# A new slot plan for banded attention followed by a gated MLP: masks of two sessions added as a bias, v of the fourth batch loaded behind its q and k, another split of one weight load

## The chip, the cores and the metric

The kernel runs on one core of a Trainium2 chip. The time is that of one execution on the device, in microseconds (us); before the change its median over three runs is 303.94 us (303.85 to 304.52). The engines are named as in the profile: PE multiplies matrices (PEld loads its weights), DVE and ACT work elementwise, POOL and SP issue DMAs here, and POOL also does a few copies.

## What is computed

Eight batches of eight heads with 576 positions of 64 dimensions go through attention in a band of 32 positions to each side; the result, as 4608 tokens of 512, goes through two matrices with a smooth ReLU between them.

```python
scores = scale * np.matmul(q, k.transpose(0, 1, 3, 2))
mask = np.abs(pos[:, None] - pos[None, :]) <= window        # window = 32
scores = np.where(mask, scores, -1000000000.0)
...
attn = attn / (np.sum(attn, axis=-1, keepdims=True) + 1e-09)
x = np.matmul(attn, v)            # as (4608, 512)
h = x @ w_in                      # (512, 2048)
g = np.where(pos, h, np.where(neg, 0.0, (h + beta) ** 2 / (4.0 * beta)))
return g @ w_out                  # (2048, 512)
```

## The kernel before

**Slots.** The program is a list of 144 slots (the loop over `a`). Each slot does one piece of the first projection: a tile `hp` of 128 x 512 sums in PSUM, either 256 of the 2048 inner columns for 256 tokens (eight matmuls of 256 columns, line 609) or, in slots 56 to 135, 128 inner columns for 512 tokens (four matmuls of 512 columns, line 630). ACT then computes `rr` from it (line 648), and the gate is finished in one of two ways: DVE does two operations (lines 654 and 655), or, for the slots listed in `two_on_act`, ACT does a square (line 651) and DVE one operation (line 652). `hp` has two buffers (pool `ps_h`), so the tile of slot a can be begun when that of slot a-2 has been read for the last time. That is after line 654 in the first way and after line 652 in the second.

**What lies between the slots.** The second projection fills PE's time. It comes as `pair` (lines 573 to 588: eight matmuls of 256 columns, numbered 0 to 15, for the first 512 tokens, placed by the list `pairs`) and as `unit` (one matmul of 512 columns, line 563, so many per slot as `units` says). Sixteen units make an output tile of 128 tokens, which is copied out of PSUM by DVE or ACT (line 567) and stored. Pairs 0, 1, 2, 3 read the four parts `('o', 0, 0, 4)` to `('o', 0, 12, 16)` of w_out; each pair also needs the gates of the slots whose inner columns it reads.

**Attention.** For batch 0 there are functions of its own (`scores`, `sums`). Batches 1 to 7 are a stream of 23 turns: `stream_scores(k)` multiplies q and k in quarters of the array (line 283), takes the exponential on ACT (lines 289, 292), multiplies by the band mask on DVE (line 200) and adds two halves into `rows` on DVE (lines 299 to 303). `stream_sums(k)` multiplies by v and by ones (line 366), ACT takes the reciprocal of the sums by a logarithm and an exponential (lines 317 to 321), and DVE multiplies into `xT` (line 325), which is what the first projection reads. Where they stand is a list of (position, names); position 12.5 lies behind the pairs and units of slot 12, position 13.0 ahead of those of slot 13. At a position listed in `ends_first` the reciprocal goes ahead of the scores that follow; elsewhere behind them. Two banks of PSUM each are held by the pools `ps_s` and `ps_n`.

**A mask in two ways.** `mask(eng, ...)` multiplies on DVE. Where `eng` is None, nothing is multiplied, and `add_mask` (line 202) has put a large negative bias into the PSUM banks by four matmuls of 512 columns ahead of the scores, which then add to it. `bias_until` is the position up to which the second way is taken; `stream_scores` knows only the first.

**Loads.** POOL issues the loads in the order of `LOADS`, written by hand: w_in in parts (`'w'`), w_out in parts (`'o'`), q and k of batch 1 (`'rows'`), v of batch 1, the two copies that make `mask4` (`'masks'`, lines 151 and 153, no DMA), and q and k of batch 2 (`'nat'`). Batch 0 and 1 are transposed by PE (`tposes`; `tq` and `tk` are those of q and k of batch 1). From batch 2 on, q and k are loaded by `load_nat` (line 103), transposed by a DMA that SP issues (`xpose`, line 193), and after the transpose of k POOL makes a copy of two columns of it into `gate` (line 668), so that the four loads of v (line 111) that are behind it are issued when that transpose has landed. The q and k of the next batch are behind them on POOL, and their buffers are those of the batch before.

The load of columns 256 to 512 of w_in into the lower 64 partitions is divided after 52 of its 64 rows.

Of the kernel before, what the change touches and what calls it, by code (L numbers as in the profile page):

```python
# [14 lines left out]
def kernel(  # L15
# [59 lines left out]
    qTs = [const.tile([128, PAD + NY * S], BF, name=f"qT{i}") for i in range(3)]  # L75

    ctx.enter_context(tc.manual_schedule())
    LOADS = [('v', 0, 1), ('v', 0, 2), ('v', 0, 3), ('w', 0, 256, 0), ('w', 0, 256, 1), ('w', 256, 512, 0), ('w', 256, 512, 1, (0, 52, 64)), ('half', 1, 0, 0), ('half', 1, 0, 1), ('half', 1, 1, 0), ('half', 1, 1, 1), ('w', 512, 768, 0), ('w', 512, 768, 1), ('w', 768, 1024, 0), ('w', 768, 1024, 1), ('w', 1024, 1280, 0), ('w', 1024, 1280, 1), ('w', 1280, 1536, 0), ('w', 1280, 1536, 1), ('w', 1536, 2048, 0), ('w', 1536, 2048, 1), ('o', 0, 0, 4), ('o', 0, 4, 8), ('o', 0, 8, 12), ('rows', 1, 0), ('rows', 1, 1), ('o', 0, 12, 16), ('v', 1, 0), ('v', 1, 1), ('v', 1, 2), ('v', 1, 3), ('masks',), ('o', 1, 0, 8), ('o', 1, 8, 16), ('nat', 2, 0), ('nat', 2, 1)]
    V, P, A = nc.vector, nc.gpsimd, nc.scalar


# [110 lines left out]

# [71 lines left out]

    def stream_scores(k, eng, pool=ps_s):

        assert eng is not None
        s, gs = turns[k]
        m = len(gs)
        r0 = (gs[0] - s) % TURN  # L270
        ps = two_banks(pool)
        sp = list(spare()) if m == 3 else None

        def place(h, y, n):
            return sp[h][:, 1, 128 * y:128 * y + 128] if n == 2 else ps[:, h, 256 * y + 128 * n:256 * y + 128 * n + 128]

        for y, n in [(y, n) for y in range(2) for n in range(min(m, 2))] + [(y, 2) for y in range(2) if m == 3]:
            for a in range(2):
                for h in range(2):
                    b, c = 1 + gs[n] // NC, gs[n] % NC  # L280
                    lo, hi = 32 * (c == 0), TAIL if c == NC - 1 else 128
                    s0 = S * (y + 2 * a) + 64 * c
                    nc.tensor.matmul(place(h, y, n)[HD[a], lo:hi], kT[b][HD[h], s0:s0 + 64],  # L283
                                     qTs[b % 3][HD[h], PAD + s0 - 32 + lo:PAD + s0 - 32 + hi],
                                     start=True, stop=True, skip_group_check=True)
        w0 = 128 * r0
        lo, hi = 32 * (gs[0] % NC == 0), 128 * m - 32 * (gs[-1] % NC == NC - 1)
        cut = min(hi, 256)
        A.activation(wt[:, :, w0 + lo:w0 + cut], ps.rearrange("p h (y j) -> p (h y) j", y=2)[:, :, lo:cut], AF.Exp,  # L289
                     scale=D ** -0.5)  # L290
        for h in (1, 0) if m == 3 else ():
            A.activation(wt[:, 2 * h:2 * h + 2, w0 + 256:w0 + hi],  # L292
                         sp[h][:, 1].rearrange("p (y j) -> p y j", y=2)[:, :, :hi - 256], AF.Exp, scale=D ** -0.5)
        mask(eng, wt[:, :, w0 + lo:w0 + hi], mask4.rearrange("p (m j) -> p m j", m=4)[:, :, lo:hi])
        M = turn_of(k)
        r = rows[64 * gs[0] - 32] = ptp.tile([128, 4, 192], BF, name="rows", bufs=2)
        if r0:
            x = wt[:, :, w0 - 64:w0 - 64 + 128 * M].rearrange("p m (n e j) -> p m n e j", n=M, e=2)
            V.tensor_add(r[:, :, :64 * M].rearrange("p m (n j) -> p m n j", n=M), x[:, :, :, 0], x[:, :, :, 1])
# [202 lines left out]

    NB = NT // TB
    NF = DFF // 256
    pairs = [(7, 0), (7, 1), (8, 2), (11, 4), (12, 5), (13, 3), (15, 8), (15, 6), (17, 9), (17, 7), (18, 10), (20, 11), (21, 14), (22, 12), (23, 15), (23, 13)]
    ev = {}

    def at(a, *todo):
# [7 lines left out]
                   "s1": (sums, 0, 1, TB, MAIN), "s2": (sums, 0, 0, MAIN, S, ps_s),  # L516
                   "tq": (tposes, 1, (0, 0), (0, 1)), "tk": (tposes, 1, (1, 0), (1, 1)),
                   "C1": (*seq[1][1], ps_n), "C3": (*seq[3][1], ps_n), "S2": (*seq[2][0], ps_s), "S0": (*seq[0][0], ps_s)}
    for a, *names in [(1, 't0'), (2, 'c0', 'c2'), (3, 'c1', 's0'), (4, 's1'), (5, 's2'), (10, 'tq'), (11.5, 'tk'), (12.5, (1, 0), 'C1'), (14.5, 'S0', (0, 1)), (15.5, (1, 2)), (19, (0, 2), (1, 3)), (21.5, (0, 3)), (24, (1, 4))]:
        for x in names:  # L520
            at(a, early_items[x] if isinstance(x, str) else seq[x[1]][x[0]])
    two_on_act = [1, 7, 10, 11, 12, 13, 25, 35, 41, 46, 53, 61, 68, 73, 75, 83, 88, 89, 90, 93, 96, 97, 104, 108, 110, 112, 113, 124, 125, 128, 129, 130, 131, 132, 133, 134, 135, 138, 139, 142, 147, 150, 152, 157]
    sl = [26.0, 29, 33, 36, 39, 44, 48, 51, 59, 66, 71, 74, 81, 87, 95, 99, 108, 111, 123]
    first_sl = 4
    bias_until = 12
    ends_first = [14, 14.5, 15.5, 16, 20, 21.5, 24.5, 27, 28, 34, 37, 38, 40, 42, 45, 46, 49, 50, 52, 54, 55, 57, 58, 62, 63, 67, 68, 69, 73, 76, 77, 78, 80, 84, 86, 88, 90, 91, 93, 94, 96, 97, 98, 101, 103, 104, 106, 110, 112, 114, 117, 120, 121, 122, 127, 130, 132, 134]
    for n, a in enumerate(sl):
# [11 lines left out]
    op = {}  # L539
# [5 lines left out]
    def unit(x):  # L545
# [70 lines left out]
    units = [0, 0, 0, 0, 0, 0, 0, 0, 0, 0, 0, 0, 0, 0, 0, 0, 0, 0, 0, 0, 0, 0, 1, 0, 0, 0, 2, 2, 5, 4, 2, 7, 2, 6, 1, 8, 7, 0, 8, 7, 2, 6, 2, 1, 5, 3, 7, 1, 6, 3, 6, 3, 4, 8, 2, 2, 2, 2, 2, 4, 4, 7, 2, 2, 2, 2, 6, 4, 5, 2, 1, 4, 2, 9, 7, 0, 9, 2, 3, 2, 2, 6, 4, 5, 2, 2, 2, 4, 4, 9, 2, 5, 0, 5, 2, 5, 5, 6, 2, 3, 4, 8, 3, 1, 3, 4, 0, 4, 6, 6, 5, 4, 3, 9, 2, 2, 2, 2, 4, 2, 8, 0, 5, 5, 0, 8, 1, 5, 0, 7, 1, 6, 1, 6, 1, 6, 1, 6, 1, 7, 3, 4, 3, 65, 2, 2, 1, 0, 0, 0, 0, 0, 0, 0, 0, 0, 0, 0, 0, 0]  # L616
    for a in range(NF * NB + 2 * NF):
        wide = WIDE[0] <= a < WIDE[1]
        for b, x in loads.get(a, []):
            load_nat(b, x)  # L620
        if a == 0 or a > 3:
            flush()
        if a < NF * NB:
# [40 lines left out]
        run(a + 0.5)  # L664
        for x in xps.get(a, []):
            xpose(*x)
            if x[1]:
                P.tensor_copy(gate, qkT(x[0], 1)[:, 0:2])  # L668
                for n in range(4):
                    load_v(x[0], n)  # L670
# [30 lines left out]
```

## Time and profile before

| what | value |
|---|---|
| median of three runs | 303.94 us |
| the profiled execution: its time | 304.81 us |
| its span, first to last instruction | 303.0 us |
| granted clock of PE | 0.999 |
| PE busy | 293.1 us (97%), 3244 matmuls |
| DVE busy | 232.0 us (77%) |
| ACT busy | 203.4 us (67%) |
| POOL busy | 78.8 us (26%) |
| DMA issued by POOL (`q0`) | 18.06 MB |

Times inside the profile count from the start of the span. A line of the timeline gives the start, the length from the first start to the modelled end of the last, the engine, the line of the kernel, output and inputs, the shape, how many instructions are merged, and in brackets how long the engine was idle before and what released it. Matmuls overlap, so the length of a row of eight (1.04 us) is longer than its distance to the next row (0.87 us); the distance between starts is what counts.

### The profile page before, as it was taken

What the parts mean: (1) busy time and instruction counts of PE and PEld (TensorE: products, weight loads), DVE (VectorE), ACT (ScalarE), POOL (GpSimd) and SP (SyncE); (2) the same over time, 40 slices, a digit from 0 to 9 for tenths busy, and PEclk for the clock granted to TensorE, in tenths of its full rate; (3) what the DMA queues carried; (4) which work ended last, traced back from release to release, by engine and by line L of the source; (5) the groups of instructions that cost most, each with busy time, mean ns of one, the idle gap of its engine ahead of it and who ended that gap; (6) DMA issues with size and microseconds to landing.
All of it is one profiled execution on the core that took longest, in us unless ns stands there. A gap on an engine that the chain in (4) does not pass through costs nothing.

```text
span 303.0 us, 7769 instructions
## 1 busy us (share of the span) xinstructions
PE 293.1 (97%) x3244; PEld 172.2 (57%) x3244; DVE 232.0 (77%) x361; ACT 203.4 (67%) x383; POOL 78.8 (26%) x98
## 2 busy tenths in 40 slices
PE   8788999999999999999999999999999999999995
PEld 3466888876665766644444444444444444446644
DVE  4269789989987889898988989688978887546700
ACT  3678696757786777766878487777578547685301
POOL 8794740090073046055046000050000000000000
PEclk9999999999999999999999999999999999999999
DMA  9999999999999999999989900697111110000121
GB/s 151 180 180 199 187 186 154 225 151 156 185 65 147 178 171 145 166 188 147 195 119 161 159 17 22 131 137 73 38 35 38 35 37 35 37 35 35 38 104 69
DMA packets 137971, 35.66 MB, mean 118 GB/s; under 512 B 122320, under 2 KB 134352, under 8 KB 137936
## 3 DMA queue, kind: packets, MB, share of 16 engines
q0 software_dynamic: 103056, 18.06, 81.0%
q1 hardware_dynamic: 34736, 16.81, 23.9%
q8 instruction: 25, 0.41, 0.6%
q10 hardware_dynamic: 144, 0.29, 0.4%
q14 instruction: 10, 0.08, 0.1%
HBM read 36.70 MB, written 9.44 MB: 152 GB/s over the span
## 4 chain that ended last, share of the span: by engine, by line
PE 82%; DMA 7%; POOL 5%; DVE 2%; ACT 2%; issue 1%; POOLq 0%; ACTq 0%; DVEq 0%
PE op L563 34%; PE hp L630 23%; PE hp L609 14%; PE op L581 4%; PE bb L366 3%; DMA w_out<-in_moe_w_out_dram 3%; DMA vn<-in_v_dram 2%; POOL w_in L116 2%; DMA w_in<-in_moe_w_in_dram 2%; POOL vn L111 2%; PE bb L283 1%; PE op L554 1%; DVE wt L200 1%; PE tp L186 1%; PE sp L366 1%
## 5 line engine op out<-in xcount | busy, mean ns | idle before, releaser
L648 ACT ACTIVATE rr<-hp 128x512 f32<-128x512 f32 x144 | 84.9, 594 | 67.0 <-PE hp L630 36.1
L563 PE MATMUL op<-w_out,gT 128*128 128x512 bf16 x496 | 125.5, 380 | 0.0
L654 DVE TENSOR_TENSOR mx<-hp,rr 128x512 f32<-128x512 f32 x104 | 71.2, 685 | 17.2 <-ACT rr L648 16.5
L630 PE MATMUL hp<-xT,w_in 128*128 128x512 bf16 x320 | 81.1, 379 | 0.0
L563 PEld LDWEIGHTS <-gT 128*128 128x128 bf16 x496 | 46.9, 98 | 49.8
L655 DVE SCALAR_TENSOR_TENSOR gT<-rr,mx 128x512 bf16<-128x512 f32 x104 | 72.2, 694 | 3.6
L609 PE MATMUL hp<-xT,w_in 128*128 128x256 bf16 x512 | 65.8, 273 | 2.6 <-DMA w_in<-in_moe_w_in_dram 1.7
L609 PEld LDWEIGHTS <-w_in 128*128 128x128 bf16 x512 | 48.9, 98 | 17.6 <-issue 3.0
L630 PEld LDWEIGHTS <-w_in 128*128 128x128 bf16 x320 | 31.3, 98 | 37.9 <-issue 0.2
L652 DVE SCALAR_TENSOR_TENSOR gT<-hp,mx 128x512 bf16<-128x512 f32 x40 | 27.5, 688 | 15.8 <-ACT mx L651 14.4
L668 POOL COPY gate<-kT 128x2 bf16<-128x2 bf16 x6 | 1.3, 224 | 113.6 <-DMA kT<-kn 113.6
L111 POOL DMA_DIRECT2D vn<-in_v_dram x32 | 27.3, 870 | 6.6 <-DVE gT L652 2.4
L651 ACT ACTIVATE mx<-rr 128x512 f32<-128x512 f32 x40 | 25.2, 630 | 1.3
L289 ACT ACTIVATE wt<-bb 128x1024 bf16<-128x1024 f32 (+2 forms) x23 | 22.1, 966 | 5.7 <-PE bb L283 5.7
L200 DVE TENSOR_TENSOR wt<-wt,mask 128x1408 bf16<-128x1408 bf16 (+4 forms) x23 | 19.5, 847 | 6.0 <-ACT wt L292 5.3
L325 DVE TENSOR_TENSOR xT<-bb,rc 128x768 bf16<-128x768 f32 (+4 forms) x25 | 20.5, 827 | 3.3 <-ACT rc L321 3.2
L567 ACT COPY osb<-op 128x512 f32<-128x512 f32 x23 | 13.3, 578 | 10.7 <-PE op L563 10.7
L321 ACT ACTIVATE rc<-rc 128x768 f32<-128x768 f32 (+4 forms) x24 | 18.3, 763 | 0.8
L581 PE MATMUL op<-w_out,gT 128*128 128x256 bf16 x128 | 16.1, 273 | 1.2 <-DMA w_out<-in_moe_w_out_dram 1.2
L103 POOL DMA_DIRECT2D qn<-in_q_dram x12 | 14.8, 1259 | 1.8 <-DMA kn<-in_k_dram 1.3
L103 POOL DMA_DIRECT2D kn<-in_k_dram x12 | 14.8, 1267 | 0.2 <-issue 0.2
L581 PEld LDWEIGHTS <-gT 128*128 128x128 bf16 x128 | 12.5, 98 | 2.8 <-issue 1.3
(82 smaller groups left out, 206.6 us busy)
## 6 DMA issues: line engine op xcount, KB each, us to landing
out_dram<-osb SPq DMA_DIRECT2D x30, 256.0 KB, 2.4
vn<-in_v_dram POOLq DMA_DIRECT2D x32, 144.0 KB, 5.0
qn<-in_q_dram POOLq DMA_DIRECT2D x12, 288.0 KB, 8.0
kn<-in_k_dram POOLq DMA_DIRECT2D x12, 288.0 KB, 9.8
out_dram<-osb SPq DMA_DIRECT2D x12, 128.0 KB, 1.7
w_in<-in_moe_w_in_dram POOLq DMA_DIRECT2D x11, 128.0 KB, 5.0
w_out<-in_moe_w_out_dram POOLq DMA_DIRECT2D x4, 256.0 KB, 9.5
w_out<-in_moe_w_out_dram POOLq DMA_DIRECT2D x2, 512.0 KB, 11.9
```

The lines of the kernel that those rows point to most:

```text
L103: nc.gpsimd.dma_start(out=x[:, :, h], in_=src[b, NY * h:NY * h + NY].rearrange("y s d -> (y s) d") .rearrange("(u p) d -> p u d", p=128))
L111: nc.gpsimd.dma_start(out=vn[b][64 * a:64 * a + 64, :, h], in_=v[b, y:y + 2].rearrange("y s d -> (y s) d") .rearrange("(c r) d -> r c d", ...
L200: eng.tensor_mul(p, p, m)
L563: nc.tensor.matmul(op[tt], gT[:, j, home(tt // 2), 128 * (tt % 2):128 * (tt % 2) + 128], w_out[:, j], start=j == 0, stop=j == 15)
L581: nc.tensor.matmul(o[:, tt], gT[:, j, p, 128 * tt:128 * tt + 128], w_out[:, j, 256 * half:256 * half + 256], start=not done, stop=len(done ...
L609: nc.tensor.matmul(hp[:, j], w_in[:, kk, 256 * f + 128 * j:256 * f + 128 * j + 128], xT[:, kk, r0:r0 + TB], start=first and n == 0, stop=l ...
L630: nc.tensor.matmul(hp.rearrange("p n t -> p (n t)"), w_in[:, kk, 128 * f:128 * f + 128], xT[:, kk, r0:r0 + 2 * TB], start=n == 0, stop=n == 3)
L648: A.activation(rr, hp, AF.Relu, scale=0.5, bias=0.5)
L651: A.activation(mx, rr, AF.Square)
L652: V.scalar_tensor_tensor(g, hp, 1.0, mx, op0=ALU.max, op1=ALU.min)
L654: V.tensor_max(mx, hp, rr)
L655: V.scalar_tensor_tensor(g, rr, 1.0, mx, op0=ALU.min, op1=ALU.mult)
```

## The change

The order of the loads: q of batch 1 and the masks go ahead of the third part of w_out, k of batch 1 stays behind it; the w_in load is divided after 50 rows in place of 52. Both lists are cut to where they differ.

```diff
-('w', 256, 512, 1, (0, 52, 64))
+('w', 256, 512, 1, (0, 50, 64))
...
-('o', 0, 0, 4), ('o', 0, 4, 8), ('o', 0, 8, 12), ('rows', 1, 0), ('rows', 1, 1), ('o', 0, 12, 16),
-('v', 1, 0), ('v', 1, 1), ('v', 1, 2), ('v', 1, 3), ('masks',), ('o', 1, 0, 8), ('o', 1, 8, 16),
+('o', 0, 0, 4), ('o', 0, 4, 8), ('rows', 1, 0), ('masks',), ('o', 0, 8, 12), ('rows', 1, 1), ('o', 0, 12, 16),
+('v', 1, 0), ('v', 1, 1), ('v', 1, 2), ('v', 1, 3), ('o', 1, 0, 8), ('o', 1, 8, 16),
```

Scores of the stream can take the mask as a bias, and two turns, 0 and 1, now do (position 12.5 and 13.0, with `bias_until` 15). Turn 1 moves from 12.5 to 13.0, the sums of turn 0 from 14.5 to 13.5.

```diff
 def stream_scores(k, eng, pool=ps_s):
-    assert eng is not None
...
+    if eng is None:
+        add_mask([ps[:, h] for h in range(2)], 4, 128)
...
-                                     start=True, stop=True, skip_group_check=True)
+                                     start=eng is not None, stop=True, skip_group_check=True)
...
...
-(12.5, (1, 0), 'C1'), (14.5, 'S0', (0, 1)), (15.5, (1, 2)), (19, (0, 2), (1, 3)), (21.5, (0, 3)), (24, (1, 4))
+(12.5, (1, 0)), (13.0, 'C1'), (13.5, 'S0'), (14.5, (0, 1)), (15.5, (1, 2)), (19, (0, 2), (1, 3)), (21.0, (0, 3)), (24.5, (1, 4))
...
-    bias_until = 12
+    bias_until = 15
```

v of batch 3 is loaded right behind q and k of batch 3, without the copy into `gate`:

```diff
+    BESIDE = [3]
...
         for b, x in loads.get(a, []):
             load_nat(b, x)
+            if x and b in BESIDE:
+                for n in range(4):
+                    load_v(b, n)
...
             xpose(*x)
-            if x[1]:
+            if x[1] and x[0] not in BESIDE:
                 P.tensor_copy(gate, qkT(x[0], 1)[:, 0:2])
```

The plan. Of `two_on_act` the slots 13, 35, 73, 88, 104, 131 and 142 go and 5, 16, 17, 38, 76 and 119 come (40 slots become 39). Of `ends_first` 21.5 goes and 1, 2, 4, 11.5, 12.5 and 123 come. `units` differs in fifteen slots; the sum is the same:

| slot | 22 | 25 | 26 | 27 | 28 | 31 | 32 | 90 | 91 | 122 | 123 | 127 | 128 | 132 | 133 |
|---|---|---|---|---|---|---|---|---|---|---|---|---|---|---|---|
| units before | 1 | 0 | 2 | 2 | 5 | 7 | 2 | 2 | 5 | 5 | 5 | 5 | 0 | 1 | 6 |
| units after | 0 | 1 | 5 | 4 | 0 | 8 | 1 | 3 | 4 | 6 | 4 | 3 | 2 | 0 | 7 |

```diff
-    pairs = [(7, 0), (7, 1), (8, 2), (11, 4), (12, 5), (13, 3), (15, 8), (15, 6), (17, 9), (17, 7), (18, 10), (20, 11), (21, 14), (22, 12), (23, 15), (23, 13)]
+    pairs = [(7, 0), (8, 1), (10, 2), (11, 4), (12, 5), (13, 3), (15, 6), (15, 9), (17, 7), (17, 8), (18, 14), (20, 10), (20, 13), (22, 11), (23, 15), (25, 12)]
...
...
-            (V.tensor_copy if tt in [15, 19, 20, 24, 25, 30, 31, 32, 35] else A.copy)(osb, op[tt])
+            (V.tensor_copy if tt in [12, 15, 19, 20, 24, 25, 28, 29, 31, 32, 33, 34, 35] else A.copy)(osb, op[tt])
```

A function `relay`, which would copy q or k of batch 1 into another layout, is added with its names and with a lookup in `tpose`; no position of the plan calls it.

More of the change, by code (lines that the diff above doesn't have):

```diff
@@ L77 @@
     ctx.enter_context(tc.manual_schedule())
-    LOADS = [('v', 0, 1), ('v', 0, 2), ('v', 0, 3), ('w', 0, 256, 0), ('w', 0, 256, 1), ('w', 256, 512, 0), ('w', 256, 512, 1, (0, 52, 64)), ('half', 1, 0, 0), ('half', 1, 0, 1), ('half', 1, 1, 0), ('half', 1, 1, 1), ('w', 512, 768, 0), ('w', 512, 768, 1), ('w', 768, 1024, 0), ('w', 768, 1024, 1), ('w', 1024, 1280, 0), ('w', 1024, 1280, 1), ('w', 1280, 1536, 0), ('w', 1280, 1536, 1), ('w', 1536, 2048, 0), ('w', 1536, 2048, 1), ('o', 0, 0, 4), ('o', 0, 4, 8), ('o', 0, 8, 12), ('rows', 1, 0), ('rows', 1, 1), ('o', 0, 12, 16), ('v', 1, 0), ('v', 1, 1), ('v', 1, 2), ('v', 1, 3), ('masks',), ('o', 1, 0, 8), ('o', 1, 8, 16), ('nat', 2, 0), ('nat', 2, 1)]
+    LOADS = [('v', 0, 1), ('v', 0, 2), ('v', 0, 3), ('w', 0, 256, 0), ('w', 0, 256, 1), ('w', 256, 512, 0), ('w', 256, 512, 1, (0, 50, 64)), ('half', 1, 0, 0), ('half', 1, 0, 1), ('half', 1, 1, 0), ('half', 1, 1, 1), ('w', 512, 768, 0), ('w', 512, 768, 1), ('w', 768, 1024, 0), ('w', 768, 1024, 1), ('w', 1024, 1280, 0), ('w', 1024, 1280, 1), ('w', 1280, 1536, 0), ('w', 1280, 1536, 1), ('w', 1536, 2048, 0), ('w', 1536, 2048, 1), ('o', 0, 0, 4), ('o', 0, 4, 8), ('rows', 1, 0), ('masks',), ('o', 0, 8, 12), ('rows', 1, 1), ('o', 0, 12, 16), ('v', 1, 0), ('v', 1, 1), ('v', 1, 2), ('v', 1, 3), ('o', 1, 0, 8), ('o', 1, 8, 16), ('nat', 2, 0), ('nat', 2, 1)]
     V, P, A = nc.vector, nc.gpsimd, nc.scalar
@@ L173, in tpose @@
         if b:
-            src = qn[b] if t == 0 else kn[b]
-            src = [src[:, half + 2 * h] for h in range(2)]
+            src = (qn, kn)[t].get((b, half))
+            src = [(qn, kn)[t][b][:, half + 2 * h] for h in range(2)] if src is None else src
             dst = qkT(b, t).rearrange("d (y e p j) -> d y e p j", y=2, e=2, j=9)[:, half, :, :, j0:j1]
@@ L189, in tpose, with relay @@
         return lambda: copy(dst, ps[:, :j1 - j0].rearrange(like, p=64 if b else 32))
+    def relay(b, t, half, copy):
+        src, nm = ((qn, "qh"), (kn, "kh"))[t]
+        x = src[b, half] = early.tile([128, 9, 2 * D], BF, name=nm, tag=nm, bufs=2)
+        copy(x.rearrange("p j (h d) -> p h j d", h=2), src[b][:, half::2].rearrange("p h (j d) -> p h j d", d=D))
     def xpose(b, t):
@@ L518 @@
                    "C1": (*seq[1][1], ps_n), "C3": (*seq[3][1], ps_n), "S2": (*seq[2][0], ps_s), "S0": (*seq[0][0], ps_s)}
-    for a, *names in [(1, 't0'), (2, 'c0', 'c2'), (3, 'c1', 's0'), (4, 's1'), (5, 's2'), (10, 'tq'), (11.5, 'tk'), (12.5, (1, 0), 'C1'), (14.5, 'S0', (0, 1)), (15.5, (1, 2)), (19, (0, 2), (1, 3)), (21.5, (0, 3)), (24, (1, 4))]:
+    for n, copy in (("V", V.tensor_copy), ("P", P.tensor_copy), ("A", A.copy)):
+        for t in range(2):
+            for half in range(2):
+                early_items[f"r{t}{half}{n}"] = relay, 1, t, half, copy
+    for a, *names in [(1, 't0'), (2, 'c0', 'c2'), (3, 'c1', 's0'), (4, 's1'), (5, 's2'), (10.0, 'tq'), (11.5, 'tk'), (12.5, (1, 0)), (13.0, 'C1'), (13.5, 'S0'), (14.5, (0, 1)), (15.5, (1, 2)), (19, (0, 2), (1, 3)), (21.0, (0, 3)), (24.5, (1, 4))]:
         for x in names:
             at(a, early_items[x] if isinstance(x, str) else seq[x[1]][x[0]])
-    two_on_act = [1, 7, 10, 11, 12, 13, 25, 35, 41, 46, 53, 61, 68, 73, 75, 83, 88, 89, 90, 93, 96, 97, 104, 108, 110, 112, 113, 124, 125, 128, 129, 130, 131, 132, 133, 134, 135, 138, 139, 142, 147, 150, 152, 157]
+    two_on_act = [1, 5, 7, 10, 11, 12, 16, 17, 25, 38, 41, 46, 53, 61, 68, 75, 76, 83, 89, 90, 93, 96, 97, 108, 110, 112, 113, 119, 124, 125, 128, 129, 130, 132, 133, 134, 135, 138, 139, 147, 150, 152, 157]
     sl = [26.0, 29, 33, 36, 39, 44, 48, 51, 59, 66, 71, 74, 81, 87, 95, 99, 108, 111, 123]
     first_sl = 4
-    bias_until = 12
-    ends_first = [14, 14.5, 15.5, 16, 20, 21.5, 24.5, 27, 28, 34, 37, 38, 40, 42, 45, 46, 49, 50, 52, 54, 55, 57, 58, 62, 63, 67, 68, 69, 73, 76, 77, 78, 80, 84, 86, 88, 90, 91, 93, 94, 96, 97, 98, 101, 103, 104, 106, 110, 112, 114, 117, 120, 121, 122, 127, 130, 132, 134]
+    bias_until = 15
+    ends_first = [1, 2, 4, 11.5, 12.5, 14, 14.5, 15.5, 16, 20, 24.5, 27, 28, 34, 37, 38, 40, 42, 45, 46, 49, 50, 52, 54, 55, 57, 58, 62, 63, 67, 68, 69, 73, 76, 77, 78, 80, 84, 86, 88, 90, 91, 93, 94, 96, 97, 98, 101, 103, 104, 106, 110, 112, 114, 117, 120, 121, 122, 123, 127, 130, 132, 134]
     for n, a in enumerate(sl):
@@ L597, in run @@
                     todo.pop()()
-            elif fn is tposes:
-                tposes(*x)
+            elif fn in (tposes, relay):
+                fn(*x)
             else:
@@ L615 @@
     done = 64
-    units = [0, 0, 0, 0, 0, 0, 0, 0, 0, 0, 0, 0, 0, 0, 0, 0, 0, 0, 0, 0, 0, 0, 1, 0, 0, 0, 2, 2, 5, 4, 2, 7, 2, 6, 1, 8, 7, 0, 8, 7, 2, 6, 2, 1, 5, 3, 7, 1, 6, 3, 6, 3, 4, 8, 2, 2, 2, 2, 2, 4, 4, 7, 2, 2, 2, 2, 6, 4, 5, 2, 1, 4, 2, 9, 7, 0, 9, 2, 3, 2, 2, 6, 4, 5, 2, 2, 2, 4, 4, 9, 2, 5, 0, 5, 2, 5, 5, 6, 2, 3, 4, 8, 3, 1, 3, 4, 0, 4, 6, 6, 5, 4, 3, 9, 2, 2, 2, 2, 4, 2, 8, 0, 5, 5, 0, 8, 1, 5, 0, 7, 1, 6, 1, 6, 1, 6, 1, 6, 1, 7, 3, 4, 3, 65, 2, 2, 1, 0, 0, 0, 0, 0, 0, 0, 0, 0, 0, 0, 0, 0]
+    units = [0, 0, 0, 0, 0, 0, 0, 0, 0, 0, 0, 0, 0, 0, 0, 0, 0, 0, 0, 0, 0, 0, 0, 0, 0, 1, 5, 4, 0, 4, 2, 8, 1, 6, 1, 8, 7, 0, 8, 7, 2, 6, 2, 1, 5, 3, 7, 1, 6, 3, 6, 3, 4, 8, 2, 2, 2, 2, 2, 4, 4, 7, 2, 2, 2, 2, 6, 4, 5, 2, 1, 4, 2, 9, 7, 0, 9, 2, 3, 2, 2, 6, 4, 5, 2, 2, 2, 4, 4, 9, 3, 4, 0, 5, 2, 5, 5, 6, 2, 3, 4, 8, 3, 1, 3, 4, 0, 4, 6, 6, 5, 4, 3, 9, 2, 2, 2, 2, 4, 2, 8, 0, 6, 4, 0, 8, 1, 3, 2, 7, 1, 6, 0, 7, 1, 6, 1, 6, 1, 7, 3, 4, 3, 65, 2, 2, 1, 0, 0, 0, 0, 0, 0, 0, 0, 0, 0, 0, 0, 0]
     for a in range(NF * NB + 2 * NF):
```

## The prediction

> **What bounds the kernel.** I read the busy times first, then the chain that ended last, then PE's timeline.
>
> ```profile
> PE 293.1 (97%) x3244; PEld 172.2 (57%) x3244; DVE 232.0 (77%) x361; ACT 203.4 (67%) x383; POOL 78.8 (26%) x98
> ...
> PE 82%; DMA 7%; POOL 5%; DVE 2%; ACT 2%; issue 1%; POOLq 0%; ACTq 0%; DVEq 0%
> ```
>
> PE is the bound; a plan can win only where PE stands still, and it pays for every matmul added. So I looked for stalls: the distance from start to start, less what the row takes where nothing waits (eight matmuls of a slot or a pair: 0.87 us).
>
> ```profile
> 25.74 1.92 PE L609 MATMUL hp<-xT,w_in 128*128 128x256 bf16 x16
> 27.49 1.04 PE L581 MATMUL op<-w_out,gT 128*128 128x256 bf16 x8
> 29.68 1.03 PE L581 MATMUL op<-w_out,gT 128*128 128x256 bf16 x8 [1.15 <-DMA w_out<-in_moe_w_out_dram]
> 30.55 1.04 PE L609 MATMUL hp<-xT,w_in 128*128 128x256 bf16 x8
> ...
> 64.34 1.05 PE L609 MATMUL hp<-xT,w_in 128*128 128x256 bf16 x8
> 65.61 1.03 PE L609 MATMUL hp<-xT,w_in 128*128 128x256 bf16 x8 [0.22 <-DVE mx L654]
> 67.07 0.28 PE L366 MATMUL bb<-rows,ones 64*64 64x192 bf16 x4 [0.42 <-DVE rows L299]
> ...
> 70.53 1.24 PE L563 MATMUL op<-w_out,gT 128*128 128x512 bf16 x5
> 71.91 1.03 PE L609 MATMUL hp<-xT,w_in 128*128 128x256 bf16 x8
> ...
> 94.45 0.27 PE L366 MATMUL bb<-wt,vn 64*64 64x32 bf16 x7
> 95.39 0.45 PE L366 MATMUL bb<-wt,vn 64*64 64x96 bf16 x24 [0.68 <-DMA vn<-in_v_dram]
> ```
>
> From 25.7 us on these are the stalls: pair 1 waits for the second part of w_out (27.49 to 29.68 less 0.87: 1.32); slot 26 waits for its PSUM buffer (0.39) and the sums behind it for `rows` (1.46 less 0.87 and 0.10 for the change of array mode: 0.49); slot 29 for DVE (1.38 less five units of 0.216: 0.30); the sums of turn 8 for v of batch 3 (0.94 for seven small matmuls that elsewhere take 0.06: 0.88). A further 0.3 lies in the sums at 43.47, which with `rows` there take 1.06 to the next slot; their matmuls, by the sums at 53.80, need 0.75. After 96 us I find none above 0.1. Ahead of 25.7 us PE waits for w_in's loads, the last of which (issued 18.70, 7.0 to landing) frees slot 6 at 25.74; no order of loads up to there changes.
>
> **The change part by part**, by walking PE, ACT and DVE on from 25.7 us with the durations of the rows.
>
> *Pairs and loads.* Slot 8 goes ahead of pair 1: it runs 28.36 to 29.23, and pair 1 still starts at 29.68, so 0.87 of the 1.32 is filled. Then slot 9 needs the buffer of slot 7, which DVE releases at 30.63: 0.1 of wait. Slot 10 follows at 31.6, and `tq` needs q of batch 1. That load now is next behind w_out's second part (landed 20.12+9.52 = 29.64); before, it landed 2.9 after the load ahead of it (33.3 against 30.4), so now at 32.5, where PE is at 32.5: 0.1 to 0.2. Pair 2 moves behind `tq`, to 33.9, when its part of w_out (33.4, 0.8 behind q) is there. k of batch 1 has the same bytes ahead of it as before and lands at 36.1 (22.32+13.8); `tk` reaches it at 36.6. Slot 11 starts at 34.72 in place of 35.27: **-0.55**; nothing of it (0) if q lands late, -0.87 if no wait is left. The two mask copies (0.29 and 1.46 on POOL) now stand ahead of five loads; POOL has about eight loads under way at all times there (the load of q of batch 2 was issued at 36.39, when the eighth before it, k of batch 1, landed at 36.1), so DMA has work while POOL copies, and I take 0; without that cover it is 1.75. v of batch 1 lands at 41.6 at the latest, ahead of its sums. The gate operation beside the mask copy (line 655 at 32.98) took 0.94 in place of 0.69; the copy now runs at 22 us, where DVE has 0.88 idle: 0. [...]
>
> *The split in 50 and 14.* The last part lands at 14.74 (8.82+5.92); some 0.1 either way, and slot 2 waits 0.7 for a later load at 18.46 anyway: 0.
>
> *Masks as a bias.* Two times four matmuls of 512 columns by quarters; that set at 21.51 put the next start at 21.75: 0.24 each, 0.48. One group of small matmuls becomes two, twice: into the mode costs 0.10 (42.50 to 43.47 for 0.87), out of it 0.13 (47.24 to 47.59 for sixteen that take 0.22 at 73.32): 0.46. DVE loses 0.63 and 0.68 and ACT nothing; with `rows` earlier the 0.3 at 43.47 goes. Net **+0.64**; bounds +0.3 (sets hide behind the wait for `kT`, which DVE copies last) and +0.94.
>
> *Slots 15 to 29.* Slots 16 and 17 get their square on ACT: their buffers come free at 50.5 and 51.7, needed at 51.1 and 52.8: 0. Copying out of pair 7 must be over for pair 14 at 52.0; ACT is done at 51.6: 0. Pair 12 and one unit move from slots 22 and 23 to slot 25, into the stall: 0.39 and 0.49 fall to nothing, but DVE comes to slot 26 with `rows` only at 66.0 and PE at 66.2, so I keep 0.03: **-0.85**; bounds -0.88 and -0.4. The 0.30 at slot 29 stays: it hangs on the exponential of turn 5, the mask, `rows`, the product and line 654 in one line, which starts as much earlier as PE does; five units more ahead of slot 28 do not shorten it.
>
> *v of batch 3.* Its four issues (3.4 us on POOL) move ahead of the gate, behind k of batch 3: at 68.9 to 72.3. They land about 80 in place of 95.35, wanted at 93.7 (94.45 less the 0.76 won by then). Queued behind them on POOL are q and k of batch 4, which wait for the transpose of k anyway (84.5); without gate and v they are issued there in place of 88.93, 4 us earlier, as is all behind them. SP's queue: the transposes of batch 3 (73.46 and 78.10) now run beside v. **-0.88**; 0 if v delays the transpose of k, which lands at 84.4, by more than 2.9 + 0.9 (its scores were at 88.08, now at 87.3).
>
> ```profile
> 78.10 2.90 SPq L193 DMA_TRANSPOSE kT<-kn  x1
> 84.55 0.18 POOL L668 COPY gate<-kT 128x2 bf16<-128x2 bf16 x1 [15.70 <-DMA kT<-kn]
> 85.58 3.41 POOL L111 DMA_DIRECT2D vn<-in_v_dram  x4 [0.85 <-PE hp L609]
> ```
>
> *ACT or DVE for squares and copies.* DVE takes over copies 12, 28, 29, 33, 34 (0.68 each), loses copy 30, and has one more operation by the squares. In each place I set the moved operation into DVE's row and compared the release with the start of the slot two later. One does not fit: copy 12 in slot 67.
>
> ```profile
> 150.93 0.69 DVE L655 SCALAR_TENSOR_TENSOR gT<-rr,mx 128x512 bf16<-128x512 f32 x1
> 151.54 0.68 DVE L652 SCALAR_TENSOR_TENSOR gT<-hp,mx 128x512 bf16<-128x512 f32 x1
> 152.79 0.69 DVE L654 TENSOR_TENSOR mx<-hp,rr 128x512 f32<-128x512 f32 x1 [0.57 <-ACT rr L648]
> ...
> 152.40 1.03 PE L630 MATMUL hp<-xT,w_in 128*128 128x512 bf16 x4
> ```
>
> The copy goes between the first two, and the second, which releases the buffer of slot 68, ends at 152.83 in place of 152.22; slot 70 started at 152.40. So **+0.42**; 0 if the copy finds a gap, 0.6 at most. Elsewhere the operation fits: slot 73 has 2.2 us of room, 35 2.3, 119 1.2, 76 0.8; in 88, 104 and 131 the release comes earlier, since line 654 releases before line 652 would; copies 28 and 29 fall into idle time of 1.4 and 0.75. The later shifts of `units` follow these: 0. `relay` is not called: 0. The end (last unit to last store) is untouched.
>
> **Sum:** -0.55 +0.64 -0.85 -0.88 +0.42 = -1.22. The profiled span of 303.0 becomes 301.8. That execution took 304.81, 0.87 more than the median of the runs; I take the difference over to the median: 303.94 - 1.22 = **302.7**. With the bounds of the five terms: -0.87+0.3-0.88-0.88 = -2.3, and 0+0.94-0.4+0+0.6 = +1.1.
>
> **Rivals.**
> 1. *All stalls go.* The early wait is filled whole, bias sets hide, and copy 12 finds a gap: -0.87+0.3-0.88-0.88 = -2.3: 301.6. For it: DVE's own idle time at 60 to 66 us; against it: DVE's row at 151 has no gap.
> 2. *The early part gives nothing*: q of batch 1 or k lands later, POOL's mask copies being ahead of further loads, and `tq` and `tk` take over the wait for w_out: -1.22+0.55 = -0.67: 303.3. For it: DMA is over 90% busy there; against it: no load has more bytes ahead except w_out's third part.
> 3. *v delays the transpose of k.* v is 576 KB; at the 150 GB/s of that stretch 3.8 us. Transposes alone took 4.9 to 6.4 to land, beside loads 5.6 to 7.0, which speaks for less than 1. If the whole 3.8 is added, k is ready at 88.2, needed at 87.3, and the 0.88 is lost: -0.34: 303.6. [...]
> 4. *DVE late (slower).* In about half of the slots the buffer is released only 0.05 to 0.25 before it is used. Eleven operations of about 0.69 enter DVE's row (five copies, six squares); I let one cost. If three more find less idle time than their length, 3 x 0.69 = 2.07: -1.22+2.07 = +0.85: 304.8. It decides where two of them stall PE (+0.16). For it: DVE is over 90% busy from 66 to 110 us; against it: from 258 us on it idles half the time.
>
> **Chances.** Forecast 0.50, rival 1 0.14, rival 2 0.17, rival 3 0.07, rival 4 0.12. The measurement of this kernel can tell about 0.2% (0.6 us) from no change. Faster by more: nearly all of the forecast, rival 1 and half of rival 2: 0.72; within: half of rival 2 and rival 3: 0.15; slower: 0.13. The range leaves out rival 4 and little else: 301.5 to 303.9; the forecast's own is 302.1 to 303.2.
>
> **What would show it.** Right: pair 1 still at about 29.7 behind slot 8, slot 11 near 34.7; slots 26 and 27 without a wait; no wait for `vn` at turn 8; POOL's `gate` copies five in place of six; eight more matmuls of line 205; a stall of 0.4 at slot 70. Wrong: a new wait of PE for `qn`, `kn` or `kT`, or waits of line 630 for DVE in several slots.

## The result and the profile after

The changed kernel takes 309.03 us (median of six runs, 307.23 to 310.3) against 303.89 (six runs, 303.18 to 304.52): the ratio is 1.016, with a 95% interval of 1.0124 to 1.0196. It is **slower by 1.6%**; the prediction had said 302.7. The profiled execution has a span of 306.9 us and a time of 308.62.

From the page of the kernel after: the busy time of each engine, the granted clock of PE in 40 slices of 7.7 us, and the chain that ended last by engine.

```profile
PE 291.9 (95%) x3221; PEld 173.5 (57%) x3252; DVE 234.4 (76%) x364; ACT 201.4 (66%) x378; POOL 79.3 (26%) x97
...
PEclk9999999999977999999999999999999999999999
...
PE 85%; DMA 8%; POOL 3%; issue 2%; DVE 1%; ACT 0%; POOLq 0%
```

PE's busy time is no longer than before (31 of its matmuls left no record: 3221 stand against 3252 weight loads), and the span has grown by 3.9: PE stands still more. Two digits of the clock are 7. Before, the mean clock was 0.999; all six runs after have 0.989 or 0.993.

To find the place, I set the start of each slot's first matmul after against the same slot before (after less before, us):

| slot | 8 | 11 | 15 | 26 | 29 | 36 | 37 | 39 | 40 |
|---|---|---|---|---|---|---|---|---|---|
| difference | -1.73 | -0.85 | -0.43 | -0.80 | -1.29 | -1.28 | +3.83 | +4.76 | +3.85 |

Up to slot 36 the new plan wins 1.28. Then 6.04 are lost within three slots and 0.9 won back; from slot 40 to the end nothing changes any more. PE's timeline after, around slots 36 to 39:

```profile
85.29 1.04 PE L621 MATMUL hp<-xT,w_in 128*128 128x256 bf16 x8
86.25 0.54 PE L373 MATMUL bb<-wt,vn 64*64 64x64 bf16 x32
...
90.15 0.59 PE L290 MATMUL bb<-qT,kT 64*64 64x96 bf16 x16 [3.18 <-DMA kT<-kn]
90.52 0.42 PE L290 MATMUL sp<-qT,kT 64*64 64x128 bf16 x8
91.28 2.77 PE L575 MATMUL op<-w_out,gT 128*128 128x512 bf16 x6 [0.33 <-issue]
93.84 2.83 PE L621 MATMUL hp<-xT,w_in 128*128 128x256 bf16 x16
96.51 1.89 PE L575 MATMUL op<-w_out,gT 128*128 128x512 bf16 x8
```

Before, the scores of turn 8 did not wait:

```profile
87.97 0.28 PE L366 MATMUL sp<-rows,ones 64*64 64x256 bf16 x4
88.08 0.37 PE L283 MATMUL bb<-qT,kT 64*64 64x96 bf16 x16
```

Two things are to be seen. After the change the scores of turn 8 wait for `kT` of batch 3 (3.36 from where PE would have begun them, at 86.79). And what follows is slow: the seven units of slot 36, six of them on record, take 2.77 where eight take 1.89 a little later. The stretches of 2 us around it, with the busy time of PE, PEld, DVE, ACT and POOL (and instructions), PE's clock, the time of the DMA packets as a share of 16 engines and GB/s:

```profile
86.00:88.00 2.00, 0.96 (x43) 0.54 (x41) 1.93 (x4) 0.60 (x1) 0.00 (x0) 1.00 1.23 262
88.00:90.00 2.00, 0.00 (x0) 0.00 (x0) 0.47 (x1) 0.00 (x0) 0.00 (x0) 0.72 0.66 231
90.00:92.00 2.00, 1.52 (x26) 1.00 (x28) 0.00 (x0) 1.21 (x3) 1.33 (x2) 0.50 0.02 9
92.00:94.00 2.00, 2.00 (x6) 0.76 (x5) 1.46 (x3) 1.93 (x5) 2.00 (x2) 0.50 1.08 69
94.00:96.00 2.00, 2.00 (x13) 1.44 (x11) 0.95 (x1) 0.21 (x1) 1.53 (x2) 0.57 2.47 149
```

In stretches of 0.25 us the clock is 1.00 up to 88.75, 0.79 in the next, 0.50 from 89.00 to 95.50, 0.55 in the next and 1.00 again from 95.75 on. With these two levels 0.72 is a fall at 88.88 and 0.57 a return at 95.72: 6.84 us at half, of which 5.57 (from 90.15) meet work. The sixteen matmuls from 93.84 take 2.67 to the next row in place of twice 0.87, 0.93 more, and half of the 1.88 up to 95.72 is 0.94; by this I estimate the cost of the 5.57 at half, 2.8. So the account of slots 36 to 40 is: 3.36 of wait, 2.7 of slow work (6.04 less 3.36), and 0.9 back for the wait for `vn` that is gone.

Why `kT` is late stands in the queues of POOL and SP. First POOL after, then SP after, then SP before, for q:

```profile
69.94 3.47 POOL L111 DMA_DIRECT2D vn<-in_v_dram  x4
...
90.67 2.45 POOL L103 DMA_DIRECT2D qn<-in_q_dram  x2 [17.26 <-DMA kT<-kn]
```

```profile
74.15 5.90 SPq L199 DMA_TRANSPOSE qT<-qn  x1
80.22 6.37 SPq L199 DMA_TRANSPOSE kT<-kn  x1
```

```profile
73.46 4.47 SPq L193 DMA_TRANSPOSE qT<-qn  x1
```

SP issues the transposes one behind the other: k's issue starts 0.17 after the end of q's, before as after, and it is longer where the landing is later (2.90 with 6.3 to the landing before, 6.37 with 9.9 after). Before, k's was issued at 78.10, and `kT` landed at 84.4. After, q's issue starts 0.7 later (it does so without the early loads too: 75.52 in experiment 1). With four loads of v beside them it lasts 1.4 longer, so k's starts 2.1 later, and it takes 9.9 to land in place of 6.3: 5.7 later in all, at 90.1. The loads of q and k of batch 4 wait for it too and leave at 90.67, not at 84.5 as forecast (before: 88.93).

### The profile page after: what moved, and what is told of

Read it like the earlier page. It is cut to its first block, busy times and chain, and to the rows that moved or that the text cites. A ratio compares the mean times of both kernels' runs of the same rounds, so it can differ in the third digit from the quotient of the medians.

```text
span 306.9 us, 7749 instructions
## 1 busy us (share of the span) xinstructions
PE 291.9 (95%) x3221; PEld 173.5 (57%) x3252; DVE 234.4 (76%) x364; ACT 201.4 (66%) x378; POOL 79.3 (26%) x97
## 4 chain that ended last, share of the span: by engine, by line
PE 85%; DMA 8%; POOL 3%; issue 2%; DVE 1%; ACT 0%; POOLq 0%
PE op L575 33%; PE hp L645 22%; PE hp L621 16%; PE op L593 5%; PE bb L373 3%; DMA kT<-kn 3%; DMA w_in<-in_moe_w_in_dram 3%; DMA vn<-in_v_dram 2%; POOL w_in L116 2%; PE bb L290 2%; PE op L566 1%; PE tp L186 1%; POOL kh L90 1%; PE sp L373 1%; PE sp L290 1%
## 5 line engine op out<-in xcount | busy, mean ns | idle before, releaser
L575 PE MATMUL op<-w_out,gT 128*128 128x512 bf16 x472 | 121.5, 382 | 3.3 <-issue 3.2
L669 DVE TENSOR_TENSOR mx<-hp,rr 128x512 f32<-128x512 f32 x105 | 72.0, 686 | 17.6 <-ACT rr L663 17.0
L670 DVE SCALAR_TENSOR_TENSOR gT<-rr,mx 128x512 bf16<-128x512 f32 x105 | 73.0, 695 | 3.6
L621 PE MATMUL hp<-xT,w_in 128*128 128x256 bf16 x512 | 66.7, 275 | 2.9 <-DMA w_in<-in_moe_w_in_dram 2.2
L206 DVE TENSOR_TENSOR wt<-wt,mask 128x1408 bf16<-128x1408 bf16 (+3 forms) x21 | 18.2, 866 | 8.6 <-ACT wt L299 7.3
L593 PE MATMUL op<-w_out,gT 128*128 128x256 bf16 x128 | 16.1, 273 | 0.0
L579 DVE COPY osb<-op 128x512 f32<-128x512 f32 x12 | 8.2, 685 | 7.6 <-PE op L575 7.6
```

Of the source, the lines that this page charges most:

```text
L575: nc.tensor.matmul(op[tt], gT[:, j, home(tt // 2), 128 * (tt % 2):128 * (tt % 2) + 128], w_out[:, j], start=j == 0, stop=j == 15)
L593: nc.tensor.matmul(o[:, tt], gT[:, j, p, 128 * tt:128 * tt + 128], w_out[:, j, 256 * half:256 * half + 256], start=not done, stop=len(done ...
L621: nc.tensor.matmul(hp[:, j], w_in[:, kk, 256 * f + 128 * j:256 * f + 128 * j + 128], xT[:, kk, r0:r0 + TB], start=first and n == 0, stop=l ...
L669: V.tensor_max(mx, hp, rr)
L670: V.scalar_tensor_tensor(g, rr, 1.0, mx, op0=ALU.min, op1=ALU.mult)
```

## Experiments

Theory A: the four loads of v beside the transposes delay `kT`, and PE's wait for it is the loss, with the clock on top. Theory B: the loss is in the rest of the plan (the other slots, the bias, DVE), and the wait for `kT` only shows it. Ratios are to the kernel before, run on the same chip; the profiles' own jitter is 1 to 2 us, most of it from PE's waits for w_in in the first 26 us (slot 6 starts between 25.65 and 27.62).

**1. The gate back for batch 3.**

```diff
-    BESIDE = [3]
+    BESIDE = []
```

> The changed kernel with the gate back for batch 3: its v is issued behind the landing of the transpose of k, as before the change; all else as changed. Theory (v's loads beside the transposes of batch 3 delay them): the wait of PE for kT at turn 8 goes, slot 36 stays 1.28 ahead of before, and the sums of turn 8 wait for vn again, by about 2 us (v lands at 95.4 to 96.5, asked for at 93.2 in place of 94.4); clock 1.0; 302.5 to 304. Rival (q and k of batch 3 came later for another reason, such as the new order of loads): kT is still late by 3, 307 to 309. Rival (DVE's additional work): later slots are still late, over 306.

Measured: 302.45 (301.96 to 303.87), ratio 0.997 [0.9944, 0.9996]; clock 0.998 in the profile. All of the loss is gone. SP's queue in this run, and then the sums of turn 8 in PE's timeline:

```profile
75.52 4.06 SPq L199 DMA_TRANSPOSE qT<-qn  x1
79.75 3.30 SPq L199 DMA_TRANSPOSE kT<-kn  x1
```

```profile
94.49 0.45 PE L373 MATMUL bb<-wt,vn 64*64 64x96 bf16 x24 [0.22 <-DMA vn<-in_v_dram]
```

`kT` lands at 84.95 and nobody waits for it. The wait for `vn`, which the early load was to remove, is 0.42 by starts, where I had expected about 2: PE is there only 0.45 earlier than before (94.00 against 94.45), not 1.28, and v, though its gate came later too (85.06 against 84.55), landed at 94.45 in place of 95.35. So the part that costs 4.8 us of span (306.9 against 302.1) could have won 0.4 to 0.9.

**2. v behind q and k, in the kernel before, and nothing else.**

```diff
             load_nat(b, x)
+            if x and b in [3]:
+                for n in range(4):
+                    load_v(b, n)
...
-            if x[1]:
+            if x[1] and x[0] not in [3]:
                 P.tensor_copy(gate, qkT(x[0], 1)[:, 0:2])
```

> The kernel before with one part of the change alone: v of batch 3 behind q and k of batch 3, without the gate. Theory: the transpose of k lands at about 89 to 90 in place of 84.4, PE waits 1 to 2 us for kT at turn 8 (88.08) and no longer for vn (-0.88); 304 to 305 if the clock holds, about 307 if it drops as in the changed kernel. Rival (v beside the transposes costs nothing, the new order of loads did it): no wait for kT, 303.0.

Measured: 310.12 (308.88 to 311.46), ratio 1.0228 [1.0173, 1.0284], 3 us more than I had expected with a lower clock; clock 0.989 to 0.994 in all four runs. SP's queue, PE's timeline, and the windows with PE's clock (columns as above):

```profile
75.40 6.28 SPq L193 DMA_TRANSPOSE qT<-qn  x1
81.85 6.01 SPq L193 DMA_TRANSPOSE kT<-kn  x1
```

```profile
91.47 0.39 PE L283 MATMUL bb<-qT,kT 64*64 64x96 bf16 x16 [3.83 <-DMA kT<-kn]
```

```profile
92.00:94.00 2.00, 1.87 (x6) 0.75 (x7) 0.59 (x1) 2.00 (x6) 2.00 (x2) 0.66 0.01 0
94.00:96.00 2.00, 2.00 (x10) 1.30 (x9) 1.75 (x3) 1.05 (x2) 2.00 (x3) 0.50 1.87 120
96.00:98.00 2.00, 2.00 (x15) 1.27 (x14) 1.30 (x3) 1.55 (x3) 0.86 (x1) 0.98 2.37 150
```

The same two transposes stretch as much without any other part of the change, and the wait (4.0 by starts) and the clock follow; from slot 36 to 39 this run loses 5.69, the wait and 1.7 more. Theory B falls. That the rest of the plan is a small gain is what experiment 1 says; this run's ratio and that of the whole change overlap.

**3. The wait filled with work.** Fifteen matmuls of w_out with itself, into PSUM that the scores then write, stand ahead of the scores of turn 8 in the changed kernel, so that PE works while `kT` is under way (one of the fifteen left no record).

```diff
+        for _ in range(15 if k == 8 else 0):
+            nc.tensor.matmul(ps[:, 0], w_out[:, 0, :128], w_out[:, 0], start=True, stop=True, skip_group_check=True)
```

> The changed kernel with fifteen matmuls of 512 columns (3.2 us of PE work whose result is overwritten) ahead of the scores of turn 8, where PE waits 3.4 us for kT. Theory (of the 5.1 us lost there about 3.4 are the wait and the rest is the clock, which is halved for 6.8 us after PE stood still): the clock stays at 1.0, the wait is the same, and the time falls by 2.5 to 3, to about 306. Rival (the lower clock has another cause, or matmuls in the wait only push the scores back): 308 to 310.

Measured: 307.18 (306.96 to 308.87), ratio 1.0143 [1.0098, 1.0187]; span 305.2, clock 0.998 to 1.0 in all four runs. PE's timeline:

```profile
87.34 3.19 PE L279 MATMUL bb<-w_out 128*128 128x512 bf16 x14 [0.16 <-issue]
91.14 0.39 PE L292 MATMUL bb<-qT,kT 64*64 64x96 bf16 x16 [0.62 <-DMA kT<-kn]
...
93.10 1.91 PE L623 MATMUL hp<-xT,w_in 128*128 128x256 bf16 x16
```

The delay stays (87.34 to 91.14: 3.8), the half clock goes: slot 37 comes 1.96 behind the scores, not 3.69 (90.15 to 93.84). From slot 36 to 39 this run loses 4.15 where the kernel after loses 6.04, with a wait 0.44 longer, so that the clock alone is worth 2.3 in the traces. By the medians it is 1.9; the intervals of the two ratios overlap, so the timed runs alone don't settle its size.

**4, 6 and 9. Fewer loads beside the transposes.** Two, three or one of the four loads of v go behind k, the others behind the gate copy:

```diff
-                for n in range(4):
+                for n in range(2):
...
-            if x[1] and x[0] not in BESIDE:
+            if x[1]:
...
-                for n in range(4):
+                for n in range(2 if x[0] in BESIDE else 0, 4):
```

> The changed kernel with two of the four loads of v of batch 3 behind its q and k and two behind the gate. Theory (the delay of the transposes grows with the bytes beside them): kT lands at about 87 to 88, PE waits 0 to 1 us for it at 86.8, the two late loads land about 92 to 94 and cost 0 to 1; clock 1.0; 302 to 304. Rival (any load of v beside the transposes delays them fully): kT at 90, 307 to 309.

> As e4_two_and_two, with three loads of v beside the transposes and one behind the gate. Theory (the delay grows with the bytes beside the transposes: the landing of kT took 5.9 from its issue with two, 9.9 with four): about 7.5 to 8.5 with three, kT at 88 to 89, PE waits 1 to 2 us for it, and whether the clock halves after such a wait is seen here; 304 to 306 without, 306 to 308 with. Rival (two loads are free, each more costs all): kT at 90, as with four. Rival (up to three are free): 302.7.

> As e4_two_and_two, with one load of v beside the transposes and three behind the gate. From the start of the transpose of q to the landing of that of k it took 9.4 to 10.9 without v beside, 11.5 to 12.1 with two loads, 13.8 with three and 16.0 with four. Theory (the delay bends at two: the first two loads cost under 1 each, the next two some 2 each): 10 to 11.5 with one, kT in time, the last v lands 0 to 0.4 after it is asked for; within 0.5 us of e4_two_and_two. Rival (each load costs the same 1.5): 11.5 or more, still no wait for kT.

Measured: with two 302.72 (301.8 to 305.15), ratio 0.9977 [0.9945, 1.0009]; with three 304.4 (303.65 to 310.08), 1.0017 [0.9981, 1.0053], the two longest of its ten runs with a mean clock of 0.993 and 0.989; with one 302.67 (301.99 to 304.42), 0.9968 [0.9939, 0.9997]. SP's queue with two, then with one, and PE's timeline with three:

```profile
74.62 5.94 SPq L199 DMA_TRANSPOSE qT<-qn  x1
80.72 3.94 SPq L199 DMA_TRANSPOSE kT<-kn  x1
```

```profile
75.22 5.02 SPq L199 DMA_TRANSPOSE qT<-qn  x1
80.40 3.37 SPq L199 DMA_TRANSPOSE kT<-kn  x1
```

```profile
87.83 0.39 PE L290 MATMUL bb<-qT,kT 64*64 64x96 bf16 x16 [1.14 <-DMA kT<-kn]
```

Over all runs, from the issue of q's transpose to the landing of k's:

| loads of v beside the pair | 0 | 1 | 2 | 3 | 4 |
|---|---|---|---|---|---|
| to the landing, us | 10.9 (before), 9.4, 9.7 | 10.5 | 11.5 to 12.2 | 13.8 | 16.0, 16.1, 16.1 |
| to the end of the pair's last packet, us | 9.0 (before), 9.0, 9.2 | 10.0 | 11.1 to 11.8 | 13.4 | 14.0, 14.0, 14.1 |

To the landing, the last two loads, 288 KB, cost 4 us. But a part of these times does not follow the loads. `kT` lands 0.5 after the pair's last packet in eight of the twelve profiles and 2.0 after it in four (before, the kernel after, experiments 2 and 3). In these four alone a packet of 16 KB of the queue `instruction` starts within 0.3 us of the pair's last packet. To the last packet, the four loads cost 5.0 in all: 1.0, 1.5, 1.9 and 0.7 one after the other. Before has the 2.0 as well, so that the 5.7 by which `kT` is later are 0.7 of later issue and 5.0 of v's loads. Of the 3.36 that PE waits, though, some 1.5 go with the place of that packet, which no run moved.

Most of the 5.0 lies ahead of the pair's first packet: it starts 1.3 to 2.0 after q's issue with no load or one beside, 1.9 to 3.7 after it with two, and 4.5 to 4.8 with three or four. The packets of the loads (`q0`) and of the transposes (`q1`) from 73.4 to 78 us, first before, then after (packets, MB, share of 16 engines):

```profile
q0 software_dynamic: 2445, 0.31, 153.6%
q1 hardware_dynamic: 920, 0.24, 71.8%
```

```profile
q0 software_dynamic: 5327, 0.67, 291.7%
```

In experiments 4 and 9, with two loads and one, neither `kT` nor `vn` is waited for (slot 40 stands 2.28 and 1.87 ahead of the kernel before). These versions and that of experiment 1 are the best here; their intervals overlap, so which of them is best stays open.

**5. Is the wait for `vn` worth removing at all?** Experiment 1 with the turn behind it two positions later, so that `vn` has time:

```diff
-    sl = [26.0, 29, 33, 36, 39, 44, ...
+    sl = [26.0, 29, 33, 36, 41, 44, ...
```

> The kernel of e1_gate_back with the sums of turn 8 and the scores of turn 9 at slot 41 in place of 39. Theory (with the gate back, v of batch 3 lands at 95 to 96, and slot 41 asks for it at about 96 to 97): no wait for vn and none for kT, 0.4 to 0.9 faster than e1_gate_back, ratio 0.992 to 0.996. Rival (the turn is as tightly placed as the buffers of the slots, and two slots later it makes slots 42 to 44 wait): no faster than e1_gate_back.

Measured: 306.59 (304.81 to 307.75, twelve runs), ratio 1.0076 [1.0045, 1.0107]. PE's timeline:

```profile
99.01 0.28 PE L290 MATMUL sp<-qT,kT 64*64 64x128 bf16 x8
101.98 1.46 PE L575 MATMUL op<-w_out,gT 128*128 128x512 bf16 x5 [2.68 <-ACT rc L327]
```

The wait for `vn` is gone and a longer one is there: the units behind the scores need an output buffer in PSUM that still holds sums of the turn, until the reciprocal (`rc`) has read them. The place of the turn is no free choice. In seven of the twelve runs the mean clock was 0.994 as well; in the profiled run, where this wait has 2.7 us, it was 1.0.

**7. The two turns without the bias**, on top of experiment 4:

```diff
-    bias_until = 15
+    bias_until = 12
```

> As e4_two_and_two, but turns 0 and 1 take their mask by multiplying on DVE, as before the change; the places of the turns stay. It prices the masks as a bias: two sets of four matmuls are worth 0.48 of PE, and DVE takes 1.31 more at 40 to 43 us. Theory (PE is the bound there, and the sums of turns 0 and 1 then wait for DVE by less than what the sets cost): 0 to 0.4 faster than e4_two_and_two. Rival (the masks on DVE make the sums at 13.5 and slots 14 and 15 wait): 0.2 to 1.2 slower.

Measured: 303.16 (302.61 to 304.94), ratio 0.9981 [0.995, 1.0013]. From slot 13 to 15 this profile loses 1.42 against before, with the bias (experiment 4) 0.54: 0.9 for the bias in the traces; the medians differ by 0.44 and the ratios by 0.0004, inside the intervals. Not settled by the times.

**8. Two and two in the kernel before**, as experiment 2 with `range(2)` and the other two loads behind the gate:

```diff
+                for n in range(2):
+                    load_v(b, n)
...
-                for n in range(4):
+                for n in range(2 if x[0] in [3] else 0, 4):
```

> The kernel before with two of the four loads of v of batch 3 behind its q and k and two behind the gate, nothing else. Theory (the rest of the plan is worth 1.3 by the slots, the loads of v 0.9): no wait for vn, 0.9 faster than before, ratio 0.996 to 0.998. Rival (the gain of e4_two_and_two is all from v's loads): as fast as e4_two_and_two.

Measured: 303.77 (302.59 to 305.01), ratio 0.9992 [0.9954, 1.0029]. The transposes start 3.6 later in this run than in the profile before (77.10 against 73.46), `kT` lands at 88.64 and is waited for 0.5; then the 0.9 at `vn` is won. The gain that the early v can have is not to be told from nothing here. Experiments 4 and 8 differ by the other parts of the change: 1.05 by the medians, 0.5 by the ratios, whose intervals overlap.

**10. The split of w_in back after 52 rows**, on top of experiment 4:

```diff
-('w', 256, 512, 1, (0, 50, 64))
+('w', 256, 512, 1, (0, 52, 64))
```

> As e4_two_and_two, with the w_in load divided after 52 of its 64 rows in place of 50, as before the change. Theory (slot 2 waits for a later load anyway, so the split moves nothing): within 0.3 us of e4_two_and_two, PE's waits for w_in as there. Rival (the split sets the start of slot 1 and with it all up to slot 6): 0.3 to 1 slower or faster, with the waits for w_in changed by as much.

Measured: 302.83 (302.32 to 304.61), ratio 0.9991 [0.9966, 1.0016], against 0.9977 with 50: no difference that these runs can tell. Its profile has a wait of 0.86 for `vn` of batch 4 at 119.57 that the profile of experiment 4 has not; the split is far from there, and why v of batch 4 came later in this run was not tried.

## Why the prediction was wrong

**The step that failed** is that v of batch 3 (the term of -0.88) lies beside the transposes at a price of "less than 1". I had the right mechanism as rival 3, with its bound (2.9 + 0.9 until PE notices), and took its chance (0.07) far too small and its price (3.8 for all of v) somewhat so. Measured, the four loads cost the pair 5.0 to its last packet (589,824 bytes at 117 GB/s, not 150), and `kT` came 5.7 later in the profile after. Three things made it so.

- The rows that I used, 4.9 to 6.4 alone against 5.6 to 7.0 beside loads, were not fit for the comparison: the landings alone hold the 0.5 or the 2.0 behind the last packet, which spreads them by 1.5.
- They are times of one transpose. In all twelve profiles SP issued k's 0.16 to 0.17 us after it was through with q's, so that `kT` has the 1.4 of q's longer issue added to the 3.6 of its own.
- They were taken beside 0.1 to 0.4 MB of loads. In the kernel after, 0.84 MB moved between q's issue and its landing.

The bound was wrong too: 0 is not the least that the term can give. Beyond 3.8 of delay each us is one that PE waits. The term of -0.88 was right by itself (no wait for `vn`, slot 40 wins 0.9), but the wait that replaced it has 3.36.

The packets do not show loads and transposes side by side from the start: from q's issue at 74.15 to 78 the loads move (0.67 MB on `q0`) and the pair does not (no packet on `q1`), and why it starts so late stays open.

**The term that was missing** is the clock. Nothing in the sum or in a rival says what a long stand-still of PE does to the work behind it; here it added 2.7 us, against 3.36 for the wait itself. The profile before, at 0.999, has no such wait to learn it from. The prediction's own sign of being wrong, a new wait of PE for `kT`, is the one that came.

**What held.** Up to slot 36 the sum without v was -0.55 +0.64 -0.85 = -0.76, and -1.28 was measured. PE's timeline after, first slots 6 to 9, then slots 26 to 29:

```profile
26.19 1.92 PE L621 MATMUL hp<-xT,w_in 128*128 128x256 bf16 x16 [1.06 <-DMA w_in<-in_moe_w_in_dram]
27.95 1.04 PE L593 MATMUL op<-w_out,gT 128*128 128x256 bf16 x8
28.82 1.04 PE L621 MATMUL hp<-xT,w_in 128*128 128x256 bf16 x8
29.69 1.04 PE L593 MATMUL op<-w_out,gT 128*128 128x256 bf16 x8
30.57 1.91 PE L621 MATMUL hp<-xT,w_in 128*128 128x256 bf16 x16
32.41 1.20 PE L186 MATMUL tp<-ident,qn 128*64 128x128 bf16 x36
...
64.81 1.04 PE L621 MATMUL hp<-xT,w_in 128*128 128x256 bf16 x8
65.78 0.28 PE L373 MATMUL bb<-rows,ones 64*64 64x192 bf16 x4
...
69.27 1.04 PE L621 MATMUL hp<-xT,w_in 128*128 128x256 bf16 x8
70.63 1.03 PE L621 MATMUL hp<-xT,w_in 128*128 128x256 bf16 x8 [0.32 <-DVE mx L669]
```

- *Pairs and loads*: pair 1 stands at 29.69 behind slot 8, as said, and `tq` at 32.41 (said: 32.5). Slot 11 won 0.85, not 0.55: slot 9 does not wait, and `tq` and pair 2 (33.53 in place of 33.9) come sooner than I had them.
- *Masks as a bias*: slots 11 to 15 lost 0.42, not 0.64; inside the bounds.
- *Slots 15 to 29*: 0.86 won, 0.85 said. Slot 26 and its sums have no wait any more, and 0.32 stays at slot 29, as forecast.
- *Copy 12*: the term of +0.42 was wrong. I put the copy of output tile 12 into slot 67; it is tile 13 that is finished there. The copy of tile 12 is in slot 61, at 143.97 on DVE, where it fits; no slot near 70 waits for DVE, and the difference in starts does not change there. The other moves between ACT and DVE cost nothing that the starts of the slots show, as forecast (rival 4, DVE late, did not come; DVE's share from 66 to 110 us, given there as over 90%, is 89%).
- *The split in 50 and 14*: nothing to be seen, as forecast (experiment 10).

Without the early v the forecast's other terms make -0.34, and experiment 1 is 0.3% faster than the kernel before (0.9 us, interval 0.1 to 1.7). The interval holds that, and also the -0.76 without the term of copy 12.

## What to carry to other kernels

Price a load that is put beside another transfer at its whole length in that transfer's queue (here 5.0 us for 576 KB), and follow the queue: where one engine issues transfers one behind the other, as SP does here, a delay of the first is a delay of the issue of the second (here 1.4 us). Take the price from rows that have as many loads queued as the new place will have. A load need not go early or late as a whole: part of it ahead and part behind the gate (here one or two of four) took the late wait away without making the early one, though the gain over no early load at all is too small for these runs to tell. Price a new wait of PE of 3 to 4 us at more than its length (here 3.36 and 2.7 more, in experiment 2 4.0 and 1.7 more), since the work behind it ran at half the clock (0.50 for 6.84 us here, for about 3.4 in experiment 2).

## What the runs showed of the hardware

- **A wait of 3.2 us was followed by half of PE's clock for 6.8 us.** Profiles with waits of PE of 1.1 to 1.6 us have a clock of 0.998 or more (1.15 before: 0.999; 1.14 in experiment 6: 1.0; 1.3 in experiment 9: 0.998; 1.6 in experiment 10: 1.0); with waits of 3.2 and 3.8 it was lower in all six and all four runs, and filling the wait with matmuls kept it at 0.998 or more in all four (experiment 3). In between it varied: seven of the twelve runs of experiment 5 (wait of 2.7 in the profile) and two of the ten of experiment 6 (1.1 in the profile) had a lower clock, and the waits of those runs are not on record. Two of the 58 runs of the kernel before beside experiments 5 to 10 had 0.994 too (306.42 and 306.56 us). In the kernel after it fell at 88.88, 1.9 us after PE's last work; in experiment 2 the windows put the fall at 92.64, 1.2 us after its wait was over, and the half clock lasted 3.4 us there, 6.84 in the kernel after. What sets the moment of the fall and its length is not shown by these runs.
- **Beside 576 KB of queued loads, a pair of transposes started late and ended 5.0 us later.** Its last packet came 14.0 us after q's issue in place of 9.0, and its first packet moved 4.7 us after the issue in place of 1.3. The cause of the late start (packets of loads and of transposes, or the two ends of the transfers) was not tried.
- **A transpose landed 0.5 or 2.0 us after its last packet.** For k of batch 3 it was 2.0 in the four profiles in which a 16-KB packet of the queue `instruction` started within 0.3 us of that last packet, and 0.5 in the other eight. That the one makes the other is not shown by a run.
